# Attention and a dense mixture of experts on one core: Strassen blocks of 768 and 1024 tokens, and the keys' sums of two heads in two PSUM banks

## The chip, the cores and the metric

One core of a Trainium2 chip runs the whole program. The metric is device time in microseconds (us) for one execution; three runs of the kernel before gave 921.0, 921.02 and 921.77 us, median 921.02 us. The engines that the text speaks of are PE (matrix multiplications, with PEld for its weight loads), DVE, ACT and POOL (elementwise work) and SP (which only issues DMAs here). PE accumulates in PSUM, which has eight banks; each holds 512 float32 values per partition.

## The reference

Random-feature attention over 4 batches, 8 heads, 576 tokens, 64 values per head and 128 features; its output, 2304 tokens by 512, goes through four experts that every token uses, weighted by normalized probabilities:

```python
q_p, k_p = phi(q * s), phi(k * s)      # exp(x @ omega.T - |x|^2/2 - max) / sqrt(128)
kv  = einsum('bhsm,bhsd->bhmd', k_p, v);  z = sum(k_p, axis=2)
x   = (q_p @ kv) / (q_p @ z + 1e-6)    # 2304 tokens x 512
p   = probs / (probs.sum(-1) + 1e-9)
out = sum over 4 experts e:  p[:, e] * (relu(x @ w1[e]) @ w2[e])   # hidden width 1024
```

## The kernel before

**Precision.** A float32 operand of the expert layers is split into a high part and a rest, both of type fp32r, and each product is three matrix multiplications: high by high, high by rest, rest by high. Attention's sums over keys use plain float32; the trace counts each float32 multiplication as two PE instructions.

**The experts' visits.** The work is a list of visits (`visits`, L443 to L448). A visit takes a block of tokens and one half of an expert's hidden width (512, in four chunks `FH`); there are `NV` = 8 halves. The first 512 tokens are visited plainly. The other 1792 tokens are two blocks, u = 1 and u = 2, of `BIG` = 896 tokens each, and their first layer is done by Strassen's scheme: `build(u)` (L641) cuts the block in two halves of n = 448 tokens, forms seven combinations of the four quarters of x and splits each (`halve`: ACT writes the high part `xbh`, DVE the rest `xbl`). `sides` forms the combinations of w1. `fast(v)` (L677) runs one visit: for two groups g of hidden columns seven products, each of six multiplications with n = 448 moving columns (L694), that is 84 a visit; then `outputs` (L573 to L580), the second layer, token tile by token tile (128 tokens): four chunks by three multiplications with 512 moving columns, so 12 for each of the seven tiles, again 84 a visit. `keep` and `both` (L700 to L707) add the products on ACT and DVE and write the hidden values `hh` and `hl`; `gather` (L582) adds an output tile into `acc` on DVE. The products of a visit stand in PE's program before its outputs, but the outputs of the first three tiles begin between the last products (`begun`).

**Attention beside the experts.** Attention of later batches is cut into small steps (`later_ticks`, L386); a loop at the end of the kernel (`emit`) places a fixed number of steps for each share of a visit. Batch 4 (its four pairs of heads) is placed in the visits of u = 1; the visits of u = 2 have no attention beside them. `sum_keys` (L307) sums over the 576 keys of a pair of heads: one multiplication with all 128 rows and 256 columns for the tails of both heads (L311, the last 64 keys of either head on 64 of the rows, with zeros and ones laid out in `vb`), then four with 128 columns for either head (L315), all into one PSUM bank; ACT (L317) and DVE (L318) write the two parts of the result.

**What sets the order.** Each engine runs its instructions in the order in which the code is written; buffers come from rings (`bufs`), so an instruction that writes a new tile of a ring waits for the last readers of the old one. PSUM is one ring of eight banks for all uses (`bank`). The attention output `raw_x` is a ring of `RING` = 1344 tokens. `build(2)` runs in the last visit of u = 1.

## Time and profile before

| | |
|---|---|
| median of three runs | 921.02 us |
| the profiled execution | 921.18 us, span 919.4 us from first to last instruction |
| PE, weight load | 902.4 us (98%), 779.5 us (85%) |
| DVE, ACT, POOL busy | 551.2 us (60%), 431.4 us (47%), 379.1 us (41%) |
| granted TensorE clock | 0.999 of full speed |
| DMA | 83.56 MB, mean 91 GB/s |

A multiplication's record is longer than the distance to the next one, because they are pipelined: 128x448 has a mean of 366 ns, but one starts about every 203 ns. The cost of a multiplication on PE is therefore read from starts, not from durations. The visits of u = 1 lie between about 304.5 and 626.7 us of the span, those of u = 2 from there to the end.

### The profile page before, as it was taken

Reading aid. Unit: us, or ns where it says so; the run is one execution under the profiler, and the core shown is the slowest. Engines: PE = TensorE matmul, PEld = TensorE weight load, DVE = VectorE, ACT = ScalarE, POOL = GpSimd, SP = SyncE. Lnnn points to the kernel's source line nnn. Section 1 sums busy time; section 2 is a strip of 40 time slices with the busy share of each in tenths; the row PEclk is TensorE's granted clock in tenths of the full one; section 3 lists DMA queues with packets and bytes.
Section 4 is the critical chain, followed back from the end, with each engine's and each line's share of the span. In section 5 each row is a group of like instructions: output and inputs, shape, how many; then the busy total and the mean of one; then the engine's idle time right before and its main releaser. Section 6 shows DMA issues by size and latency. Waiting matters only on the chain.

```text
span 919.4 us, 13210 instructions
## 1 busy us (share of the span) xinstructions
PE 902.4 (98%) x4892; PEld 779.5 (85%) x4892; DVE 551.2 (60%) x945; ACT 431.4 (47%) x964; POOL 379.1 (41%) x296
## 2 busy tenths in 40 slices
PE   7999999999999999999999999999999999999998
PEld 7888887878887888888888889888888888888886
DVE  5665666776769665565666574877345545535543
ACT  4554566655655455435454445354444242343330
POOL 3856454443534443423434323445333433444330
PEclk9999999999999999999999999999999999999999
DMA  6664444444420523214123212215112122121102
GB/s 170 164 193 152 132 129 138 154 139 138 158 81 24 165 88 98 72 32 132 41 63 98 70 30 63 61 55 147 47 47 71 47 68 69 46 70 58 35 12 80
DMA packets 47360, 83.56 MB, mean 91 GB/s; under 512 B 8704, under 2 KB 17088, under 8 KB 47296
## 3 DMA queue, kind: packets, MB, share of 16 engines
q1 hardware_dynamic: 47056, 82.43, 29.8%
q8 instruction: 38, 0.62, 0.3%
q10 hardware_dynamic: 240, 0.30, 0.1%
q14 instruction: 26, 0.21, 0.1%
HBM read 77.99 MB, written 4.72 MB: 90 GB/s over the span
## 4 chain that ended last, share of the span: by engine, by line
PE 79%; DVE 10%; ACT 6%; issue 2%; DMA 1%; POOL 1%; SPq 0%; ACTq 0%; DVEq 0%; POOLq 0%
PE g L694 28%; PE g L578 12%; PE g L580 12%; PE g L579 12%; DVE dn L364 2%; PE g L563 2%; PE g L564 2%; PE g L565 2%; PE kv L315 2%; DVE acc L591 1%; ACT qp L297 1%; DVE raw_x L368 1%; PE q_ps L266 1%; ACT kp L297 1%; PE k_ps L266 1%
## 5 line engine op out<-in xcount | busy, mean ns | idle before, releaser
L578 PE MATMUL g<-w2h,hh 128*128 128x512 f32 x536 | 212.6, 397 | 0.0
L475 POOL TENSOR_TENSOR w2l<-w2r,w2h 128x512 fp32r<-128x512 f32 x93 | 122.2, 1318 | 217.9 <-ACT w2h L472 156.7
L580 PE MATMUL g<-w2h,hl 128*128 128x512 f32 x536 | 209.6, 391 | 0.8 <-DVE hl L570 0.8
L579 PE MATMUL g<-w2l,hh 128*128 128x512 f32 x536 | 209.0, 390 | 0.0
L475 POOL TENSOR_TENSOR w1sl<-w1r,w1sh 128x1024 fp32r<-128x1024 f32 (+1 forms) x59 | 113.2, 1922 | 152.9 <-ACT w1sh L472 138.1
L591 DVE SCALAR_TENSOR_TENSOR acc<-g,pr,acc 128x512 f32<-128x512 f32 x126 | 93.8, 748 | 66.2 <-PE g L580 65.3
L705 DVE TENSOR_TENSOR sum<-g,sum 128x448 f32<-128x448 f32 x96 | 59.7, 622 | 111.7 <-PE g L694 108.8
L475 POOL TENSOR_TENSOR w1al<-w1r,w1ah 128x256 fp32r<-128x256 f32 (+1 forms) x77 | 82.4, 1088 | 99.9 <-ACT w1ah L472 97.6
L580 PEld LDWEIGHTS g<-w2h,hl 128*128 128x128 f32 x536 | 100.6, 188 | 23.9 <-DVE hl L570 1.7
L578 PEld LDWEIGHTS g<-w2h,hh 128*128 128x128 f32 x536 | 100.7, 188 | 20.8 <-issue 1.4
L579 PEld LDWEIGHTS g<-w2l,hh 128*128 128x128 f32 x536 | 100.8, 188 | 18.6
L706 ACT ACTIVATE hh<-sum 128x448 fp32r<-128x448 f32 x96 | 55.5, 578 | 122.8 <-DVE sum L705 122.8
L707 DVE SCALAR_TENSOR_TENSOR hl<-sum,hh 128x448 fp32r<-128x448 f32 x96 | 61.8, 644 | 62.0 <-ACT hh L706 62.0
L472 ACT ACTIVATE w1sh<-w1r 128x1024 fp32r<-128x1024 f32 (+1 forms) x59 | 51.1, 867 | 100.0 <-DVE w1r L529 99.8
L694 PE MATMUL g<-xbh,w1sh 128*128 128x448 f32 x256 | 93.7, 366 | 0.7 <-ACT sum L700 0.7
L694 PE MATMUL g<-xbl,w1sh 128*128 128x448 f32 x256 | 93.7, 366 | 0.0
L694 PE MATMUL g<-xbh,w1sl 128*128 128x448 f32 x256 | 93.4, 365 | 0.0
L700 ACT ACTIVATE sum<-g 128x448 f32<-128x448 f32 x96 | 51.7, 541 | 56.2 <-PE g L694 56.0
L694 PE MATMUL g<-xbh,w1ah 128*128 128x448 f32 x192 | 70.6, 368 | 0.8 <-ACT kp L297 0.8
L694 PE MATMUL g<-xbh,w1al 128*128 128x448 f32 x192 | 70.3, 366 | 0.0
L694 PE MATMUL g<-xbl,w1ah 128*128 128x448 f32 x192 | 70.1, 365 | 0.0
L472 ACT ACTIVATE w2h<-w2r 128x512 fp32r<-128x512 f32 x90 | 55.7, 626 | 5.2 <-DMA w2r<-in_w 4.0
(158 smaller groups left out, 1597.1 us busy)
## 6 DMA issues: line engine op xcount, KB each, us to landing
w1r<-in_w SPq DMA_DIRECT2D x54, 512.0 KB, 3.6
w2r<-in_w SPq DMA_DIRECT2D x108, 256.0 KB, 2.7
out<-acc SPq DMA_DIRECT2D x18, 256.0 KB, 2.6
va<-in_vn SPq DMA_DIRECT2D x14, 256.0 KB, 4.7
k<-in_kd SPq DMA_DIRECT2D x12, 288.0 KB, 3.1
k<-in_kn SPq DMA_DIRECT2D x12, 288.0 KB, 4.4
q<-in_qd SPq DMA_DIRECT2D x12, 288.0 KB, 4.3
q<-in_qn SPq DMA_DIRECT2D x12, 288.0 KB, 4.7
```

The lines of the kernel that those rows point to most:

```text
L266: nc.tensor.matmul(ps[j][:, cs], t[rows, cs], om_r[rows], start=True, stop=True)
L472: hi.activation(a, t, AF.Copy)
L475: lo.tensor_tensor(c, t, f32(a), ALU.subtract)
L578: nc.tensor.matmul(ps, ha[:, ts_], wa, start=(c == 0), stop=False)
L579: nc.tensor.matmul(ps, ha[:, ts_], wc, start=False, stop=False)
L580: nc.tensor.matmul(ps, hc[:, ts_], wa, start=False, stop=(c == FH - 1))
L591: nc.vector.scalar_tensor_tensor(acc[i], ps, sc, acc[i], ALU.mult, ALU.add)
L694: nc.tensor.matmul(ps, a[:, w], x[:, k], start=(start and k + at == 0), stop=(k == 1 and at == 2), skip_group_check=not start)
L700: nc.scalar.activation(t, P_[g][where], AF.Copy)
L705: nc.vector.tensor_tensor(t, P_[g][where], t, ALU.add)
L706: nc.scalar.activation(ha, t, AF.Relu)
L707: nc.vector.scalar_tensor_tensor(hc, t, 0.0, f32(ha), ALU.max, ALU.subtract)
```

## The change

- The blocks have 768 tokens (u = 1, from token 512) and 1024 tokens (u = 2, from token 1280). A product's moving operand has 384 columns in u = 1 and 512 in u = 2; the number of products, of multiplications in each, and of output tiles over both blocks (6 + 8 where it was 7 + 7) is the same.
- In u = 2 the hidden values of the second 512 tokens live in tiles that attention used before (`k`, `q`, `kp`, `qp`), and the eighth accumulator in a tile of `qt`. To make room, the ring of attention output has 1280 tokens, the first block's two parts share one tile, and the query tails have one buffer where they had two.
- In `build`, the rest of combinations 3 and 4 is written by POOL where DVE wrote it.
- `sum_keys` has a bank for each head. The tails are two multiplications, each on its head's 64 rows with 128 columns, one into each bank; then the four of each head as before. ACT and DVE evacuate each bank by itself.
- The rate of attention steps in u = 1 follows the smaller number of tiles.

```diff
@@ exp_tails (Halves), exp (Pair)
-            f = att.tile([P, 1, M], F32, tag=which + "pt", name=which + "p", bufs=2)
+            f = att.tile([P, 1, M], F32, tag=which + "pt", name=which + "p", bufs=2 if which == "k" else 1)
...
@@ finish
-                x_first[self.hp] = [xop([P, START], x) for x in ("xh", "xl")]
+                both = xop([P, 2, START], "x_first")
+                x_first[self.hp] = both[:, 0], both[:, 1]
@@ sum_keys
-            kv = bank("kv")[:, :VZ]
-            nc.tensor.matmul(kv, self.kp[2][:, 0], vb[:, self.hp], start=True, stop=False)
+            kv = [bank("kv")[:, :P] for _ in range(2)]
+            cs = [slice((1 - j) * P, (2 - j) * P) for j in range(2)]
             for j in range(2):
-                cs = slice((1 - j) * P, (2 - j) * P)
+                rows = slice(j * D, (j + 1) * D)
+                nc.tensor.matmul(kv[j], self.kp[2][rows, 0], vb[rows, self.hp, cs[j]], start=True, stop=False)
+            for j in range(2):
                 for t in range(4):
-                    nc.tensor.matmul(kv[:, cs], self.kp[j][:, t], va[:, t, cs], start=False, stop=(j == 1 and t == 3))
+                    nc.tensor.matmul(kv[j], self.kp[j][:, t], va[:, t, cs[j]], start=False, stop=(t == 3))
             self.kv_h, self.kv_l = (att.tile([P, VZ], F32R, tag=x, name=x, bufs=1) for x in ("kvh", "kvl"))
-            nc.scalar.activation(self.kv_h, kv, AF.Copy, scale=1.0 / M)
-            nc.vector.scalar_tensor_tensor(self.kv_l, kv, 1.0 / M, f32(self.kv_h), ALU.mult, ALU.subtract)
+            for j in range(2):
+                hi, lo = self.kv_h[:, cs[j]], self.kv_l[:, cs[j]]
+                nc.scalar.activation(hi, kv[j], AF.Copy, scale=1.0 / M)
+                nc.vector.scalar_tensor_tensor(lo, kv[j], 1.0 / M, f32(hi), ALU.mult, ALU.subtract)
@@ visits
-    BIG = 7 * P
+    BIG = {1: (START, 6 * P), 2: (START + 6 * P, 8 * P)}
-    visits += [visit(u, n, START + (u - 1) * BIG, BIG) for u in (1, 2) for n in range(NV)]
+    visits += [visit(u, n, *BIG[u]) for u in (1, 2) for n in range(NV)]
@@ build
-            split(t, *X[p], nc.scalar, nc.vector)
+            split(t, *X[p], nc.scalar, nc.gpsimd if p in (3, 4) else nc.vector)
@@ fast
-        u, n = visits[v][0], BIG // 2
-        tiles = BIG // P
-        hs = [tuple(held([P, 2 * n], x) for x in ("hh", "hl")) for _ in range(FH)]
+        u, _, _, _, n = visits[v]
+        tiles, n = n // P, n // 2
+        if u == 1:
+            whole = [tuple(held([P, 2 * n], x) for x in ("hh", "hl")) for _ in range(FH)]
+            hs = [[tuple(x[:, j * n:(j + 1) * n] for x in pair) for pair in whole] for j in range(2)]
+        else:
+            wide = [att.tile([P, 2, n], F32R, tag=x, name="h_" + x, bufs=1) for x in "kq"]
+            late = [tuple(x[:, i] for i in range(2)) for x in wide]
+            late += [tuple(att.tile([P, n], F32R, tag=x, name="h_" + x, bufs=2) for _ in range(2)) for x in ("kp", "qp")]
+            hs = [[tuple(held([P, n], x) for x in ("hh", "hl")) for _ in range(FH)], late]
...
@@ emit
-            N0: (chain(opening(later[-NP]), later_ticks(later[-NP:])), 54 / (NV * (BIG // P + 1) * 0.8)),
+            N0: (chain(opening(later[-NP]), later_ticks(later[-NP:])), 54 / (NV * 7 * 0.8)),
```

**The end of the products in a visit of u = 1, on PE.** The last product of a visit stands beside the outputs of a tile (`g` is a PSUM bank, `xbh` and `xbl` the split combination of x, `w1sh` and `w1sl` that of w1). Before:

```order
L694 MATMUL g_3616<-xbh,w1sh 128x448
L694 MATMUL g_3616<-xbl,w1sh 128x448
L694 MATMUL g_3616<-xbh,w1sl 128x448
L578 MATMUL g_3696<-w2h,hh 128x512
L579 MATMUL g_3696<-w2l,hh 128x512
L580 MATMUL g_3696<-w2h,hl 128x512
```

and now:

```order
L712 MATMUL g_3644<-xbh,w1sh 128x384
L712 MATMUL g_3644<-xbl,w1sh 128x384
L712 MATMUL g_3644<-xbh,w1sl 128x384
L585 MATMUL g_3724<-w2h,hh 128x512
L586 MATMUL g_3724<-w2l,hh 128x512
L587 MATMUL g_3724<-w2h,hl 128x512
```

The order is the same, and only the width of the products has changed, to 384 here and to 512 in u = 2; there are 672 of either width where there were 1344 of 448.

**The sum over keys of a pair, on PE**, between the multiplications of a plain visit (the numbers behind `kv` tell banks apart, `kp` are the keys' features, `va` and `vb` the values and ones). Before:

```order
L565 MATMUL g1_1256<-xh_543,w1al_1048 128x512
L311 MATMUL kv_1288<-vb_77,kp_1206 128x256
L315 MATMUL kv_1288<-va_76,kp_1180 128x128 x4
L315 MATMUL kv_1288<-va_76,kp_1201 128x128 x4
L563 MATMUL g1_1304<-xh_427,w1sh_1086 128x512
```

and now:

```order
L570 MATMUL g1_1252<-x_first_540,w1al_1044 128x512
L315 MATMUL kv_1284<-vb_77,kp_1202 128x128
L315 MATMUL kv_1285<-vb_77,kp_1202 128x128
L318 MATMUL kv_1284<-va_76,kp_1176 128x128 x4
L318 MATMUL kv_1285<-va_76,kp_1197 128x128 x4
L568 MATMUL g1_1304<-x_first_427,w1sh_1082 128x512
```

The two multiplications of the tails work on 64 rows each, and stand one behind the other ahead of those with all rows; nothing has moved past another stage.

**POOL in the last visit of u = 1** (rests of the split weights, `w1al`, `w1sl`, `w2l`). Before:

```order
L475 TENSOR_TENSOR w1al<-w1r,w1ah 128x512
L475 TENSOR_TENSOR w1al<-w1r,w1ah 128x256
L475 TENSOR_TENSOR w1sl<-w1r,w1sh 128x1024 x2
L475 TENSOR_TENSOR w2l<-w2r,w2h 128x512 x4
```

and now:

```order
L480 TENSOR_TENSOR w1al<-w1r,w1ah 128x512
L480 TENSOR_TENSOR w1al<-w1r,w1ah 128x256
L480 TENSOR_TENSOR w1sl<-w1r,w1sh 128x1024
L480 TENSOR_TENSOR xbl<-raw_x,xbh 128x1024
L480 TENSOR_TENSOR w1sl<-w1r,w1sh 128x1024
L480 TENSOR_TENSOR xbl<-raw_x,xbh 128x1024
L480 TENSOR_TENSOR w2l<-w2r,w2h 128x512 x4
```

Two splits of x stand in POOL's queue, one ahead of the second `w1sl` and one ahead of the four `w2l`; they are gone from DVE's.

## Rows read from the trace of the kernel before

**Rows 1.** The page: span, and PE's busy time, share, instructions.

```profile
span 919.4 us, 13210 instructions
...
PE 902.4 (98%) x4892; PEld 779.5 (85%) x4892; DVE 551.2 (60%) x945; ACT 431.4 (47%) x964; POOL 379.1 (41%) x296
```

**Rows 2.** Windows: length, busy of PE, PEld, DVE, ACT, POOL, clock, DMA.

```profile
304.50:626.70 322.20, 320.72 (x1649) 277.20 (x1649) 207.12 (x341) 152.23 (x319) 124.47 (x89) 1.00 0.25 76
590.00:630.00 40.00, 39.47 (x184) 33.99 (x183) 32.01 (x40) 20.09 (x33) 18.39 (x12) 1.00 0.27 79
626.70:915.40 288.70, 288.70 (x1345) 252.11 (x1343) 138.16 (x220) 108.36 (x194) 105.68 (x75) 1.00 0.20 59
```

**Rows 3.** Waits of PE: in total us, times, longest us.

```profile
PE qt_ps L326 <- ACT qp L297: 2.2, 3, 1.3
...
PE nd L356 <- DVE qtl L337: 1.2, 3, 0.8
...
PE g L694 <- ACT kp L297: 0.8, 1, 0.8
PE g L694 <- ACT sum L700: 0.7, 2, 0.5
```

**Rows 4.** The chain in time: start, length of a stretch, products in it.

```profile
382.89 13.63 PE g L694 x66
...
626.84 13.38 PE g L694 x66
```

**Rows 5.** Timeline of PE, 256 columns: first and last of 22.

```profile
56.43 0.28 PE L565 MATMUL g<-xh,w1sl 128*128 128x256 f32 x1
...
58.94 0.28 PE L565 MATMUL g<-xh,w1al 128*128 128x256 f32 x1
```

**Rows 6.** Timeline of PE, 320 columns: first of six, and what follows.

```profile
132.03 0.31 PE L354 MATMUL nd<-qth,kvh 128*128 128x320 f32 x1
...
132.91 0.39 PE L578 MATMUL g<-w2h,hh 128*128 128x512 f32 x1
```

**Rows 7.** Timeline of PE, 512 columns and w1: first and last of 13.

```profile
283.85 0.39 PE L565 MATMUL g<-xh,w1al 128*128 128x512 f32 x1
...
286.57 0.39 PE L565 MATMUL g<-xh,w1sl 128*128 128x512 f32 x1
```

**Rows 8.** Timeline of PE around one sum over keys.

```profile
97.24 0.39 PE L565 MATMUL g<-xh,w1al 128*128 128x512 f32 x1
97.47 0.59 PE L311 MATMUL kv<-vb,kp 128*128 128x256 f32 x2
97.89 1.95 PE L315 MATMUL kv<-va,kp 128*128 128x128 f32 x16
99.60 0.47 PE L563 MATMUL g<-xh,w1sh 128*128 128x512 f32 x1
99.91 0.39 PE L564 MATMUL g<-xl,w1sh 128*128 128x512 f32 x1
```

**Rows 9.** Timeline of PE around multiplications on 64 rows.

```profile
91.84 0.39 PE L565 MATMUL g<-xh,w1sl 128*128 128x512 f32 x1
92.16 1.16 PE L266 MATMUL q_ps<-om_r,q 64*128 64x128 f32 x16
93.25 0.50 PE L563 MATMUL g<-xh,w1sh 128*128 128x512 f32 x1
93.59 0.39 PE L564 MATMUL g<-xl,w1sh 128*128 128x512 f32 x1
```

**Rows 10.** Lines by form: busy us, mean ns, idle before, releaser.

```profile
L694 PEld LDWEIGHTS g<-xbh,w1sh 128*128 128x128 f32 x256 | 48.1, 188 | 6.3 <-ACT sum L700 1.4
...
L317 ACT ACTIVATE kvh<-kv 128x256 fp32r<-128x256 f32 x12 | 4.6, 380 | 1.4 <-PE kv L315 1.2
...
L318 DVE SCALAR_TENSOR_TENSOR kvl<-kv,kvh 128x256 fp32r<-128x256 f32 x12 | 5.1, 424 | 16.5 <-ACT kvh L317 16.5
...
L475 DVE TENSOR_TENSOR xbl<-raw_x,xbh 128x896 fp32r<-128x896 f32 x10 | 14.1, 1417 | 6.8 <-ACT xbh L472 6.8
...
L475 POOL TENSOR_TENSOR w1sl<-w1r,w1sh 128x1024 fp32r<-128x1024 f32 x32 | 78.3, 2446 | 127.6 <-ACT w1sh L472 113.3 <-DVE acc L591 10.5 <-PE g L579 3.9
```

More of the change, by code (lines that the diff above doesn't have):

```diff
@@ L34, in attention_moe @@
     QS = float(D) ** -0.25
-    RING = 1344
+    RING = 1280
     START = 4 * P
@@ L158, in exp @@
             else:
-                f = att.tile([P, n, M], F32, tag=which + "p" + size, name=which + "p", bufs=2)
+                f = att.tile([P, n, M], F32, tag=which + "p" + size, name=which + "p", bufs=1 if which + size == "qt" else 2)
             for i in range(n):
@@ L573, in outputs @@
     def outputs(v, hs, ps, t, cs):
+        at = t * P // hs[0][0][0].shape[1]
+        hs, t = hs[at], t - at * hs[0][0][0].shape[1] // P
         ts_ = slice(t * P, (t + 1) * P)
@@ L587, in gather @@
         if n_tiles[i] == 1:
-            acc[i] = held([P, DM], "acc", F32)
+            if t < 7:
+                acc[i] = held([P, DM], "acc", F32)
+            else:
+                acc[i] = att.tile([P, DM], F32, tag="qt", name="acc")
             nc.scalar.activation(acc[i], ps, AF.Copy, scale=sc)
@@ L623, in plain @@
             ps = bank("g2")
-            outputs(v, hs, ps, t, range(2))
+            outputs(v, [hs], ps, t, range(2))
             if v == N0 - 2 and t in (0, 2):
@@ L629, in plain @@
             yield 0.5
-            outputs(v, hs, ps, t, range(2, FH))
+            outputs(v, [hs], ps, t, range(2, FH))
             gather(v, ps, t)
@@ L641, in build @@
     def build(u):
-        c0, n = START + (u - 1) * BIG, BIG // 2
+        c0, n = BIG[u]
+        n //= 2
         o = [(c0 + j * n - START) % RING for j in range(2)]
@@ L677, in fast @@
     def fast(v):
-        u, n = visits[v][0], BIG // 2
-        tiles = BIG // P
-        hs = [tuple(held([P, 2 * n], x) for x in ("hh", "hl")) for _ in range(FH)]
+        u, _, _, _, n = visits[v]
[3 more added lines that the diff above has]
+            hs = [[tuple(x[:, j * n:(j + 1) * n] for x in pair) for pair in whole] for j in range(2)]
+        else:
+            wide = [att.tile([P, 2, n], F32R, tag=x, name="h_" + x, bufs=1) for x in "kq"]
+            late = [tuple(x[:, i] for i in range(2)) for x in wide]
+            late += [tuple(att.tile([P, n], F32R, tag=x, name="h_" + x, bufs=2) for _ in range(2)) for x in ("kp", "qp")]
+            hs = [[tuple(held([P, n], x) for x in ("hh", "hl")) for _ in range(FH)], late]
         P_ = [{}, {}]
@@ L702, in both @@
         def both(g, f, j, where, name):
-            ha, hc = (x[:, j * n:(j + 1) * n] for x in hs[2 * g + f])
+            ha, hc = hs[j][2 * g + f]
             t = P_[g][name]
@@ L730, in p4 @@
             product(g, 4, "u", start=False)
-            ha, hc = (x[:, :n] for x in hs[2 * g + 1])
+            ha, hc = hs[0][2 * g + 1]
             nc.scalar.activation(ha, P_[g]["u"], AF.Relu)
@@ L927, in first_visit @@
             ps = bank("g2")
-            outputs(0, hs, ps, t, range(FH))
+            outputs(0, [hs], ps, t, range(FH))
             gather(0, ps, t)
```

## The prediction

> **What bounds the kernel now.** The page comes first: PE is busy for 902.4 of 919.4 us [rows 1], so only two things can move the end by much: how long PE needs for its own stream, or new waits in it. The windows say where the slack lies. In u = 2 PE is busy for all of its 288.7 us; in u = 1 it is idle for 322.20 - 320.72 = 1.48 us; DVE, the next engine, is busy for 207 of those 322 us [rows 2]. The waits of PE are short: the longest kinds in the stages that the change touches add up to 2.2, 1.2, 0.8 and 0.7 us [rows 3]. So no wait is there to be removed, and the change is worth what it does to the distance between starts of PE's instructions, less what it adds in waits. I therefore went from busy time to the timeline and read starts, since records of pipelined multiplications overlap.
>
> **The products' width.** 1344 products of 448 columns become 672 of 384 and 672 of 512: the same columns, and the same number of instructions. Whether that costs nothing, gives or takes depends on what a start costs beyond its columns. The granted clock is 1.00 [rows 2], the level of 2.4 GHz, at which 448 columns need 186.7 ns. The chain holds 66 products in 13.38 us, 202.7 ns each, so 16.0 ns lie on top [rows 4]. For other widths: 256 columns, 21 steps in 2.51 us, 119.5 ns, 12.8 on top of 106.7 [rows 5]; 320 columns, 6 steps in 0.88 us, 146.7 ns, 13.4 on top [rows 6]; 512 columns, 12 steps in 2.72 us, 226.7 ns, 13.4 on top of 213.3 [rows 7]. The last group has w1 standing and x moving, as the products have, so it is the right row for the new 512. The width of 448 stands out by 2.6 ns.
>
> For 384 no row exists. By the neighbours 320 and 512 it takes 160.0 + 13.4 = 173.4 ns; with the surplus of 448 it takes 176.0 ns. It is 64 columns from 320 and 64 from 448, so I take the middle, 174.7 ns. Before: 1344 x 202.7 ns = 272.4 us. After: 672 x 174.7 ns + 672 x 226.7 ns = 117.4 + 152.3 = 269.7 us. That is -2.7 us, all of it on PE, which is the path; the ends are -3.6 us (173.4 ns) and -1.8 us (176.0 ns). A further end, at which the 512 columns too carry 16.0 ns, is 0 and is a rival below. One stretch of u = 1 runs at 13.63 us for 66 products [rows 4], 3.8 ns more each; I don't know why. Two visits at that pace cost 2 x 84 x 3.8 ns = 0.6 us, which may stay or go; I count nothing for it.
>
> The outputs stay at 12 multiplications for a tile and 14 tiles over both blocks, and cost what they did.
>
> **The tails of the keys' sums.** Before, the multiplication with 256 columns takes the path from 97.47 to 97.89, 0.42 us [rows 8]. The new two have 64 rows and 128 columns, the form of the projection of queries: there 16 instructions take 1.09 us, 0.068 us each, and the new two are four instructions, 0.27 us [rows 9]. But the projection also pays at its edges. The step into it is 92.16 - 91.84 = 0.32 us, where a step behind 512 columns is 0.23: 0.09 us more. The step after it is 0.34, 0.11 more; a sum over keys, which has all 128 rows, has 0.31 there, 0.08 more [rows 8, 9], so leaving the 64 rows is worth 0.03. With both edges the new tails take 0.09 + 0.27 + 0.03 = 0.39 us. That saves 0.03 us in each of 12 pairs, -0.4 us. The ends: no edge paid, 12 x (0.27 - 0.42) = -1.8 us; the whole 0.11 paid on leaving, 12 x (0.47 - 0.42) = +0.6 us. I take the middle value, since the row has the form of the new instructions and shows the edge.
>
> The Trainium skill, TensorEngine Tiling (Array Packing), Key Properties, says the same against this edit: "Changing tiling mode (not just tile) drains the TensorE". The trace agrees, with the 0.09 us of the step in; without that rule and that row the sum would hold -1.8 us here instead of -0.4.
>
> **The two banks.** ACT's evacuation (380 ns for 256 columns) becomes two of 128, DVE's (424 ns) likewise [rows 10]. Each piece costs between half and all of the old one, so ACT gets 0 to 0.38 us and DVE 0 to 0.42 us more a pair. They lie beside PE's work: the sum is first read in `numerators`, three steps later, behind two transposing steps and expert multiplications. Value 0; if that cover were gone, up to 0.8 us a pair. A pair now takes 12 tiles of the ring of eight banks where it took 11, while a visit of u = 1 takes one fewer for its outputs. Queued behind a product that waits for a bank is all of PE.
>
> **The splits moved to POOL.** In the last visit of u = 1 DVE is the busiest helper (32.0 of 40 us in 590 to 630) and POOL has 18.4 of 40 [rows 2]. Two rests, 1.42 us each on DVE, leave it; on POOL a rest of 1024 elements takes 2.45 us [rows 10]. Behind the first stands the second `w1sl`, which the eighth product of the next visit reads: seven products, 7 x 6 x 0.2267 = 9.5 us after that visit's start, and that covers 2.45 us. The rests themselves are read by the ninth and tenth product. The four `w2l` behind them are read by outputs later still. Value 0, in `build(1)` too; without the cover 2.45 us once or twice.
>
> **Denser visits of u = 1.** A visit loses 84 x 28 ns = 2.35 us of products and a tile of 12 x 0.2267 = 2.72 us, so u = 1 shrinks by about 41 to 282 us, with the same attention and weights beside it. DVE's 207 us would be at most 73% of that, from 64%. PE's idle 1.48 us there [rows 2] may vanish or double: -1.5 to +1.5 us. I take +0.3, a fifth more, for the higher density. The buffers that become single (query tails) or shared (first block, hidden values in attention's tiles) are rewritten one pair or visit after their last read, behind PE's own later work: 0.
>
> **Sum.** -2.7 - 0.4 + 0.3 = -2.8 us. The profiled execution took 921.18 us (span 919.4 and 1.8 around it), so 918.4 us; it lies 0.16 above the median of the runs, which puts the forecast at 918.2 us. With ends of its terms near each other its own range is 916.8 to 919.6.
>
> **Rivals.**
> - *Columns alone count.* What lies on top belongs to the products, not to 448: 384 and 512 both carry 16.0 ns, 672 x (176.0 + 229.3) = 272.4 us, a gain of 0; the time is 921.0 - 0.4 + 0.3 = 920.9 us. For it: only the products have the 16 ns. Against it: the 512 columns with w1 standing carry 13.4 [rows 7]. Chance 0.17. The Trainium skill, TensorE: Matmul & The Clock Gate, Back-to-back issue gap, gives a gap of columns at 2.4 GHz plus a fixed 2.5 ns for the warm array; by that rule 384 and 512 cost on average what 448 does, and this rival holds. The rows disagree with it in size (12.8 to 16.0 ns) and in being fixed.
> - *Both gains whole.* 384 as its neighbours and the tails without edges: -3.6 - 1.8 = -5.4, 915.6 us. Rows 9 speak against the second half. Chance 0.14.
> - *The half rows do nothing.* The edges eat the tails (+0.6), the rest as forecast: 919.2 us. Chance 0.05.
> - *A wait for banks.* A product in u = 1 finds its bank still held by features that ACT has not finished; one such wait is 0.8 us now [rows 3]. If each of 12 pairs pays it for the additional bank: +9.6, 918.2 + 9.6 = 927.8 us. It ends on the slower side from (2.8 + 1.8) / 12 = 0.4 us a pair. Against it: one such wait in the whole run now, and one output bank fewer a visit. Chance 0.06.
> - *Weight loads become the bound.* A load's record is 188 ns [rows 10], just under the 202.7 of a product; if loads set the pace, 384 stays at 202.7: 672 x 28 ns = +18.8, 937 us. It ends slower once 384 takes 181.5 ns or so. Against it: with the same kind of load 256 columns start every 119.5 ns [rows 5]. Chance 0.03.
>
> **How the numbers follow.** The forecast has 0.55. A measurement of this kernel tells 0.2%, 1.84 us, from no change, so faster begins at 919.2 us. The forecast is below that in about four of five of its cases (0.44); with the whole gains (0.14), half of the third rival and a little of the first that makes 0.62 faster. The first rival, the rest of the forecast and of the third make 0.29 within, and the two last 0.09 slower. A range of 915.2 to 921.4 leaves out the two slow rivals (0.09) and the far side of the whole gains.
>
> **What would show it.** In the changed trace 66 products of u = 1 should stretch over 66 x 174.7 ns = 11.5 us (11.4 to 11.6), and those of u = 2 over 15.0 us; 15.1 and 11.6 mean the first rival, 13.4 in u = 1 the weight loads. From the start of the tails to that of the sums with all rows it should be 0.27 to 0.30 us, after a step of 0.32 into them. PE's waits in u = 1 should stay under 3 us in all, u = 2 without any, and no wait should name `xbl` on POOL. Wrong is the forecast if the 448 columns' 16 ns turn up at 512 too, or if PE's waits there grow by more than 2 us.

## The result, and the profile after

The changed kernel takes 932.21 us (median of six, 930.48 to 936.32) against 921.38 us for the kernel before in the same comparison (six, 920.86 to 924.14): ratio 1.012, 95% interval 1.0093 to 1.0147. The prediction said 918.2 us and put slower at 0.09. The profiled execution after took 930.67 us with a span of 928.9 us; the one before had 919.4 us [rows 1].

The page of the kernel after, span and busy time of each engine:

```profile
span 928.9 us, 13300 instructions
PE 904.0 (97%) x4916; PEld 769.6 (83%) x4916; DVE 554.1 (60%) x953; ACT 430.8 (46%) x976; POOL 390.2 (42%) x300
```

PE's busy time is about what it was (904.0, before 902.4), and the span is 9.5 us longer: 7.9 us of that are idle time of PE. The windows say where (columns as in [rows 2]):

```profile
302.50:555.00 252.50, 246.78 (x1394) 218.96 (x1393) 162.11 (x294) 124.82 (x289) 104.97 (x78) 1.00 0.27 84
555.00:605.00 50.00, 44.73 (x206) 38.57 (x206) 42.25 (x50) 24.63 (x40) 29.89 (x15) 0.97 0.28 86
605.00:925.00 320.00, 320.00 (x1407) 263.75 (x1405) 145.78 (x221) 111.74 (x187) 102.61 (x74) 1.00 0.17 51
573.00:575.00 2.00, 2.00 (x8) 2.00 (x7) 1.49 (x2) 0.67 (x3) 2.00 (x1) 0.50 0.00 0
```

From 605 us on PE is never idle. In the 50 us around the border between u = 1 and u = 2 it is idle for 5.3 us, and in the 252 us before that for 5.7 us. The fourth row lies inside the second one: a busy PE at a granted clock of 0.50, the level of 1.2 GHz. No stretch of u = 1 or u = 2 in [rows 2] is below 1.00.

PE's waits in the kernel after (columns as in [rows 3]):

```profile
PE g L712 <- ACT sum L718: 5.4, 5, 2.1
PE g L712 <- DVE sum L723: 2.5, 1, 2.5
PE g L585 <- DVE raw_x L373: 1.6, 1, 1.6
PE t_ps L274 <- DVE raw_x L373: 1.1, 1, 1.1
```

Before, a product waited for ACT's `sum` for 0.7 us in all [rows 3]; it is 5.4 now. The chain gives the pace of the products (columns as in [rows 4]), one stretch of u = 1 and one of u = 2:

```profile
373.75 11.45 PE g L712 x66
...
638.32 14.96 PE g L712 x66
```

That is 173.5 ns for 384 columns and 226.7 ns for 512, against 202.7 for 448 [rows 4]: 672 x 173.5 + 672 x 226.7 = 268.9 us, 3.5 us less than 272.4.

To see which visits lost time I took the distance between the first products of neighbouring visits (us; the eighth is the distance to the first visit of u = 2). The first product of u = 1 starts at 301.89 us before and at 300.78 after. "Planned" is the row of before less 84 x 29.2 ns and 12 x 0.2267 us, 5.17 us a visit:

| visit of u = 1 | 1 | 2 | 3 | 4 | 5 | 6 | 7 | 8 | sum |
|---|---|---|---|---|---|---|---|---|---|
| before | 38.48 | 42.36 | 42.45 | 42.67 | 43.02 | 40.77 | 37.82 | 37.22 | 324.8 |
| planned | 33.31 | 37.19 | 37.28 | 37.50 | 37.85 | 35.60 | 32.65 | 32.05 | 283.4 |
| after | 35.31 | 37.50 | 38.46 | 38.30 | 38.91 | 36.27 | 32.69 | 37.37 | 294.8 |

So 11.4 us of the shrinking did not come: 5.3 in the eighth visit, 2.0 in the first, 4.0 spread over the others. In u = 2 a visit was to take 36.11 + 84 x 24.0 ns + 2.72 = 40.85 us; the first takes 42.56 and the seven others 40.99, so 2.7 us more than planned in all. With 1.1 us less ahead of u = 1 (the start of the program differs by some us from profile to profile) the difference of the spans is closed: -3.5 + 11.4 + 2.7 - 1.1 = +9.5 us.

**The eighth visit, its border.** Timeline of the kernel after around 558 us, from the outputs of the visit before into the new products (start, length, engine, line, out<-in, tile; in brackets the idle time before it and its releaser), by engine:

```profile
557.29 2.67 POOL L480 TENSOR_TENSOR w1sl<-w1r,w1sh 128x1024 fp32r<-128x1024 f32 x1 [8.55 <-ACT w1sh L477]
...
557.29 0.41 DVE L531 TENSOR_TENSOR w1r<-w1r 128x256 f32<-128x256 f32 x1
557.74 2.50 DVE L532 TENSOR_TENSOR w1r<-w1r 128x256 f32<-128x256 f32 x1
...
560.73 0.43 DVE L534 TENSOR_TENSOR w1r<-w1r 128x256 f32<-128x256 f32 x1
...
561.25 1.06 ACT L477 ACTIVATE w1sh<-w1r 128x1024 fp32r<-128x1024 f32 x1 [4.04 <-DVE w1r L534]
562.22 0.47 ACT L718 ACTIVATE sum<-g 128x384 f32<-128x384 f32 x1
...
558.22 0.33 PE L712 MATMUL g<-xbh,w1ah 128*128 128x384 f32 x1
...
562.74 0.44 PE L712 MATMUL g<-xbh,w1sh 128*128 128x384 f32 x1 [1.21 <-ACT sum L718]
```

Four engines form one chain. DVE adds the quarters of the next w1 (L531 to L534); one of the four additions takes 2.50 us instead of 0.42 while POOL writes `w1sl`: it ends at 560.24, 0.28 us after POOL's instruction (559.96). That is the rule in this trace: of the 128 additions of w1, 16 take 0.60 to 2.51 us; each of them started while a POOL instruction was running and ended 0.28 to 0.29 us after it. The other 112 take 0.41 to 0.43. DVE is held here, not slowed. ACT's split of the result (L477) waits for the last addition. ACT's copy of the first product (L718) needs nothing of that, but stands behind the split in ACT's queue. And PE's fourth product of the visit adds onto the bank that this copy reads, so PE stops. Three products of six multiplications each pass before the fourth, 18 x 173.5 ns = 3.1 us; the copy starts 4.0 us after the visit's first product. Less the 2.1 us for which the addition was held it would be 1.9 (an estimate from these rows), inside the 3.1. The same chain costs 2.12 us in the first visit of u = 1 and 1.28 in the first of u = 2, and there too an addition is held (1.41 us at 301.84, 1.96 at 595.13).

The same border in the kernel before:

```profile
585.74 0.41 DVE L526 TENSOR_TENSOR w1r<-w1r 128x256 f32<-128x256 f32 x1
...
587.62 1.06 ACT L472 ACTIVATE w1sh<-w1r 128x1024 fp32r<-128x1024 f32 x1 [5.19 <-DVE w1r L529]
590.94 0.55 ACT L700 ACTIVATE sum<-g 128x448 f32<-128x448 f32 x1 [2.25 <-PE g L694]
...
589.46 0.36 PE L694 MATMUL g<-xbh,w1ah 128*128 128x448 f32 x1
```

There the additions start 3.7 us ahead of the visit's first product (0.9 after), the split is over before that product starts, and ACT's copy waits for PE, not PE for ACT.

**The eighth visit, the second block.** DVE and PE a little later, in the kernel after:

```profile
565.12 2.31 DVE L663 TENSOR_TENSOR t_k<-raw_x 128x1024 f32<-128x1024 f32 x1
567.46 2.20 DVE L663 TENSOR_TENSOR t_q<-raw_x,t_k 128x1024 f32<-128x1024 f32 x1
...
571.19 0.55 DVE L723 TENSOR_TENSOR sum<-g,sum 128x384 f32<-128x384 f32 x1
...
571.79 0.44 PE L712 MATMUL g<-xbh,w1ah 128*128 128x384 f32 x1 [2.54 <-DVE sum L723]
...
572.35 0.52 PE L712 MATMUL g<-xbh,w1al 128*128 128x384 f32 x1
572.67 0.52 PE L712 MATMUL g<-xbh,w1ah 128*128 128x384 f32 x1
```

Two combinations of x for the second block stand in DVE's queue ahead of the sums that free PE's banks, 4.5 us long where the two took 3.1 before (1.08 and 2.06). Their size is the smaller part of it: a subtraction of 1024 elements that POOL does not hold takes 1.22 us (at 572.80), one of 896 took 1.08. Before, POOL held one of the two, and now it holds both, with two `w2l` (564.73 to 568.58). PE waits 2.54 us, and then the multiplications start 0.32 us apart instead of 0.174: this is the window at 0.50 above. Twelve at that distance take 12 x 0.146 = 1.75 us more; whether the visit is longer by it, the fourth experiment shows.

**The sum over keys.** In the kernel after, beside [rows 8]:

```profile
406.31 0.39 PE L587 MATMUL g<-w2h,hl 128*128 128x512 f32 x1
406.63 0.49 PE L315 MATMUL kv<-vb,kp 64*128 64x128 f32 x4
407.05 2.05 PE L318 MATMUL kv<-va,kp 128*128 128x128 f32 x16
...
409.18 0.39 PE L586 MATMUL g<-w2l,hh 128*128 128x512 f32 x1
```

From the last multiplication ahead of the block to the second behind it: 2.87 us, before 2.67. The step in is 0.32 instead of 0.23, the tails take 0.42 as they did, and from there to the second multiplication behind the block it is 2.13 instead of 2.02, since the 16 sums take 0.10 more. Together that is +0.20 us a pair, and for 12 pairs +2.4 us. Ten of the 12 pairs show it so; at 194.73 us the tails take 0.75, and behind the pair at 119.91 PE waits:

```profile
123.14 0.38 PE L568 MATMUL g<-x_first,w1ah 128*128 128x256 f32 x1 [0.76 <-ACT qp L298]
```

The expert's multiplication reads nothing of `qp`; by the code only the ring of banks ties it to ACT's exponentials.

### The profile page after: what moved, and what is told of

It is laid out like the page before. It is cut to its first block, busy times and chain, and to the rows that moved or that the text cites. A ratio compares the mean times of both kernels' runs of the same rounds, so it can differ in the third digit from the quotient of the medians.

```text
span 928.9 us, 13300 instructions
## 1 busy us (share of the span) xinstructions
PE 904.0 (97%) x4916; PEld 769.6 (83%) x4916; DVE 554.1 (60%) x953; ACT 430.8 (46%) x976; POOL 390.2 (42%) x300
## 4 chain that ended last, share of the span: by engine, by line
PE 77%; DVE 11%; ACT 6%; issue 3%; POOL 1%; DMA 0%; ACTq 0%; DVEq 0%; POOLq 0%
PE g L712 27%; PE g L585 12%; PE g L587 11%; PE g L586 11%; PE g L568 2%; PE g L569 2%; PE g L570 2%; DVE dn L369 2%; PE kv L318 2%; DVE acc L601 1%; ACT qp L298 1%; PE q_ps L267 1%; PE k_ps L146 1%; DVE raw_x L373 1%; PE k_ps L267 1%
## 5 line engine op out<-in xcount | busy, mean ns | idle before, releaser
L585 PE MATMUL g<-w2h,hh 128*128 128x512 f32 x408 | 162.4, 398 | 1.6 <-DVE raw_x L373 1.6
L587 PE MATMUL g<-w2h,hl 128*128 128x512 f32 x408 | 159.6, 391 | 0.3 <-DVE hl L575 0.3
L723 DVE TENSOR_TENSOR sum<-g,sum 128x384 f32<-128x384 f32 (+1 forms) x96 | 59.7, 622 | 108.7 <-PE g L712 103.7
L712 PE MATMUL g<-xbh,w1sh 128*128 128x384 f32 (+1 forms) x256 | 93.6, 366 | 5.6 <-ACT sum L718 5.4
L477 ACT ACTIVATE w1sh<-w1r 128x1024 fp32r<-128x1024 f32 (+1 forms) x59 | 51.1, 867 | 97.7 <-DVE w1r L534 97.6
L712 PE MATMUL g<-xbl,w1sh 128*128 128x384 f32 (+1 forms) x256 | 93.0, 363 | 0.0
L712 PE MATMUL g<-xbh,w1sl 128*128 128x384 f32 (+1 forms) x256 | 92.9, 363 | 0.0
L718 ACT ACTIVATE sum<-g 128x384 f32<-128x384 f32 (+1 forms) x96 | 51.5, 539 | 64.2 <-PE g L712 63.6
L712 PE MATMUL g<-xbh,w1ah 128*128 128x384 f32 (+1 forms) x192 | 70.3, 366 | 2.8 <-DVE sum L723 2.5
L712 PE MATMUL g<-xbh,w1al 128*128 128x384 f32 (+1 forms) x192 | 69.9, 364 | 0.0
L712 PE MATMUL g<-xbl,w1ah 128*128 128x384 f32 (+1 forms) x192 | 69.8, 363 | 0.0
L712 PEld LDWEIGHTS g<-xbh,w1sh 128*128 128x128 f32 x256 | 48.3, 189 | 13.5 <-ACT sum L718 7.2
```

Source lines behind the costliest of these rows:

```text
L477: hi.activation(a, t, AF.Copy)
L585: nc.tensor.matmul(ps, ha[:, ts_], wa, start=(c == 0), stop=False)
L587: nc.tensor.matmul(ps, hc[:, ts_], wa, start=False, stop=(c == FH - 1))
L712: nc.tensor.matmul(ps, a[:, w], x[:, k], start=(start and k + at == 0), stop=(k == 1 and at == 2), skip_group_check=not start)
L718: nc.scalar.activation(t, P_[g][where], AF.Copy)
L723: nc.vector.tensor_tensor(t, P_[g][where], t, ALU.add)
```

## The experiments

Each ratio is against the kernel before, run on the same chip; the kernel after has 1.012.

**One bank again** (`e1_one_bank`): the changed kernel with the old `sum_keys`.

```diff
-            kv = [bank("kv")[:, :P] for _ in range(2)]
...
+            kv = bank("kv")[:, :VZ]
+            nc.tensor.matmul(kv, self.kp[2][:, 0], vb[:, self.hp], start=True, stop=False)
```

> The changed kernel with the sum over keys of before: one bank, one multiplication of 128 rows and 256 columns for the tails. Theory edges (the step into and out of the 64 rows costs PE 0.20 us a pair: the block from the last expert multiplication ahead of it to the second behind it takes 2.87 us in the changed kernel and 2.67 before): 12 x 0.20 = 2.4 us faster than the changed kernel, nothing else moves. Theory ring (the twelfth bank of a pair makes PE meet banks that DVE's divisions still hold: 1.6 + 1.1 us of waits on raw_x, which before had none): these 2.7 us go as well, 5.1 us in all. Rival (both are chance of placement): 0 to 1 us. The 5.4 us of waits on ACT's copies of product sums stay by all three.

931.94 us, ratio 1.012 (1.0106 to 1.0135): no difference that can be told. In its trace u = 1 is 294.1 us long (after 294.8), 0.18 us for each of its four pairs, and every wait of PE above is still there with its length, the 2.5 us and the two of `raw_x` among them. So the additional bank is not their cause. It moves a wait in the plain visits: the 0.76 us behind the second pair are gone here, and those of `qt_ps` for ACT's `qp` are 2.3 us, as before (2.2), where the kernel after has 0.9. All PE's waits from 90 to 295 us add up to 3.7 us here and 3.2 in the kernel after.

**Two banks alone** (`e2_two_banks_alone`): the kernel before with the new `sum_keys` and nothing else (the same lines with the signs exchanged).

```diff
-            kv = bank("kv")[:, :VZ]
+            kv = [bank("kv")[:, :P] for _ in range(2)]
```

> The kernel before with the new sum over keys alone (blocks stay 896 and 896). Theory edges: 12 x 0.20 = 2.4 us slower than before, 923.8 us, with PE's waits as before. Theory ring: waits on raw_x or other evacuations appear beside it, some 2 to 3 us more. The prediction's step (0.03 us a pair saved): 0.4 us faster.

922.67 us against 920.96, ratio 1.0018 (1.0009 to 1.0027): slower by 1.7 us. The pair of [rows 8] in its timeline:

```profile
96.48 0.39 PE L569 MATMUL g<-xh,w1al 128*128 128x512 f32 x1
96.80 0.49 PE L314 MATMUL kv<-vb,kp 64*128 64x128 f32 x4
97.22 2.05 PE L317 MATMUL kv<-va,kp 128*128 128x128 f32 x16
...
99.35 0.39 PE L568 MATMUL g<-xl,w1sh 128*128 128x512 f32 x1
```

2.87 us again. The half rows cost time in either kernel, and that they should save 0.4 us falls. The wait behind the second pair is there too (0.77 us), and PE's idle time in u = 1 stays at 1.5.

**The sums of w1 group by group, two steps sooner** (`e3_sides_early`).

```diff
...
+        for i in range(2):
+            direct(i)
+            yield
+            add(i)
+            yield
+            summed(i)
+            yield
@@ fast
         p7(1)
+        next(ready, None)
@@
         begun(2)
+        next(ready, None)
```

> The changed kernel with the combinations of the next visit's w1 made group by group and two steps sooner (direct, add, summed of group 0, two of them between the last products; then those of group 1 in the first three output tiles). Theory border (at the end of a visit of six tiles ACT stands at the split of w1sh, waiting for DVE's adds, with the copy of the first product of the next visit queued behind it, and PE's third product waits for that copy): the waits of 2.1, 1.2 and 1.3 us at the starts of visits go, about 5 us faster than the changed kernel. Rival (DVE has too much to do in those places, wherever the adds stand): the waits move to sums or hidden values, less than 1.5 us gained.

939.54 us, ratio 1.0208 (1.0192 to 1.0223): a miss in the total. The eighth visit shrank from 37.37 to 34.72 us and the first of u = 2 from 42.56 to 41.20, as the chain would have it, but the fourth grew from 38.30 to 42.57, where PE waits 3.4 us for `raw_x`, and the first from 35.31 to 39.05, where the wait for ACT's `sum` stays (2.2) and DMAs of `k` and `q` are waited for (1.1 and 0.8). Too much moved at once.

**Rests of combinations 3 and 4 on DVE again** (`e4_halves_dve`).

```diff
-            split(t, *X[p], nc.scalar, nc.gpsimd if p in (3, 4) else nc.vector)
+            split(t, *X[p], nc.scalar, nc.vector)
```

> The changed kernel with all rests of x's combinations on DVE, none on POOL. Theory pool (POOL's rests lengthen DVE's instructions beside them: a DVE add of w1 took 1.96 to 2.50 us there instead of 0.43): DVE gets shorter in all, and 1 to 3 us are gained at the start of u = 2. Rival (DVE is the short engine there, POOL has time): two rests of 1.2 to 2.6 us come back to DVE, and the first visits of u = 1 and u = 2 lose 1 to 3 us.

930.82 us, ratio 1.0108 (1.0094 to 1.0122). The medians do not tell it from the kernel after, but the trace does: the first visit of u = 1 takes 33.77 us instead of 35.31, the other visits what they took. The rests on POOL cost that border 1.5 us: beside them DVE's third rest took 2.59 us (here 0.95) and the first addition of w1 1.41 (here 0.41). The rest of 2.51 us ahead of these is as long here, beside POOL's `w1sl`.

Its eighth visit settles what the slow clock cost (timeline of PE, and the window of the fourth row above):

```profile
571.86 0.44 PE L712 MATMUL g<-xbh,w1ah 128*128 128x384 f32 x1 [2.54 <-DVE sum L723]
...
573.00:575.00 2.00, 1.93 (x11) 1.45 (x9) 1.56 (x2) 0.67 (x2) 2.00 (x1) 1.00 0.00 0
```

The wait is the same 2.54 us, the granted clock behind it is 1.00, and the visit takes 37.38 us, as in the kernel after (37.37). PE is through the next products sooner and waits 0.61 and 0.66 us for ACT instead of 0.24. So the slow clock lay over time that PE would have waited anyway.

**A higher rate of attention steps in the kernel before** (`e5_rate_before`).

```diff
-            N0: (..., 54 / (NV * (BIG // P + 1) * 0.8)),
+            N0: (..., 54 / (NV * (BIG // P + 1) * 0.7)),
```

> The kernel before with one number changed: attention's steps are placed in u = 1 at 54 / (8 x 8 x 0.7) = 1.21 a share, the changed kernel's rate, instead of 1.05; blocks stay 896 and 896. Theory density (what makes PE wait in u = 1 of the changed kernel is how many steps stand beside one output tile): waits on raw_x and on ACT's copies turn up in u = 1, 2 to 4 us slower than before. Rival (the shorter products are what uncovers them, the steps don't matter): within 1 us of before.

924.09 us against 920.69, ratio 1.0032 (1.002 to 1.0044): +3.4 us with wide products, all seven tiles and one bank. Its waits:

```profile
PE g L694 <- ACT sum L700: 1.5, 2, 1.0
PE t_ps L273 <- DVE raw_x L368: 1.1, 1, 1.1
```

The wait for `raw_x` of 1.1 us is that of the kernel after. So density has a price of its own, which the prediction put at 0.3.

**A lower rate in the kernel after** (`e6_rate_after`).

```diff
-            N0: (..., 54 / (NV * 7 * 0.8)),
+            N0: (..., 54 / (NV * 7 * 0.87)),
```

> The changed kernel with the steps placed at 54 / (8 x 7 x 0.87) = 1.11 a share instead of 1.21. Theory density: the waits of 1.1 and 1.6 us on raw_x go, 2 to 3 us faster than the changed kernel, unless the last steps run into the build of the second block. Rival (short products): unchanged within 1 us.

937.2 us, ratio 1.0172 (1.0146 to 1.0199): slower, a miss for density as the whole story. The waits for `raw_x` went down to 0.6 us, but those of products grew:

```profile
PE g L712 <- ACT sum L718: 10.6, 6, 3.0
```

Three visits that had no wait at their fourth product now wait 2.96, 2.49 and 1.23 us there. So what counts seems to be which steps fall on a border; which ones did here was not followed up.

**The additions of w1 on POOL** (`e7_adds_pool`), for the visits of u = 1.

```diff
+            eng = nc.gpsimd if N0 < v <= N0 + NV else nc.vector
-            nc.vector.tensor_tensor(r22, r21, r22, ALU.add)
+            eng.tensor_tensor(r22, r21, r22, ALU.add)
```

(and so the three lines that follow)

> The changed kernel with the adds that combine w1 on POOL for the visits prepared during u = 1 (eight adds of 128x256 a visit, 0.43 us each on DVE when nothing slows them). Theory DVE short (DVE's queue at the output tiles is what ACT's split of w1sh and the release of banks wait for): the waits on raw_x and part of those on ACT's copies go, 3 to 6 us faster than the changed kernel. Rival (it is the chain from adds over ACT to PE, or DVE and POOL slowing each other): POOL takes about 0.8 us for each add, the split comes later still, 0 to 5 us slower.

934.83 us, ratio 1.0146 (1.013 to 1.0163). Products now wait 8.8 us for ACT's `sum`, and the second visit takes 42.44 us instead of 37.50, the first of u = 2 45.43 instead of 42.56; others are shorter, the eighth at 34.79. On POOL an addition takes 0.74 to 0.80 us in the mean. At the second border ACT's split starts at 340.48 us, 1.7 us behind the visit's first product, and exponentials of attention stand between it and the copy at 344.80. Moved to POOL, the additions are no way out.

**One combination of the second block later** (`e8_less_later`).

```diff
         p1(1)
-        next(more, None)
         p2(1)
+        next(more, None)
```

> The changed kernel with one step of the second block's build moved in the last visit of u = 1, from ahead of the second product of group 1 to behind it, so that the two first subtractions (2.31 and 2.20 us on DVE) no longer stand together ahead of that product's sum. Theory queue (those 4.5 us make the wait of 2.54 us on DVE's sum, and the clock's drop to 1.2 GHz behind it): that wait and the slow products behind it go, 3 to 4 us faster than the changed kernel. Rival (the work is only put off): the wait moves to the seventh product or the hidden values, under 1 us gained.

930.7 us, ratio 1.0109 (1.0091 to 1.0127). The eighth visit takes 36.30 us instead of 37.37. PE's waits there:

```profile
571.21 0.44 PE L712 MATMUL g<-xbh,w1ah 128*128 128x384 f32 x1 [1.45 <-DVE sum L723]
...
574.89 0.49 PE L585 MATMUL g<-w2h,hh 128*128 128x512 f32 x1 [0.63 <-ACT hh L750]
...
576.74 0.44 PE L712 MATMUL g<-xbh,w1sh 128*128 128x384 f32 x1 [0.67 <-ACT sum L718]
```

The wait for DVE's `sum` falls from 2.54 to 1.45 us, and the granted clock stays at 1.00. But the products that now run at full pace meet waits of 0.63 and 0.67 us right behind, where the kernel after had 0.24. So 1.1 us are gained, which is what the wait lost: as in the fourth experiment, the slow clock had lain over waits that come without it.

**One step sooner** (`e9_step_sooner`): the next visit's weights are advanced once more in each visit of u = 1, ahead of its outputs, and by one step in the last plain visit.

```diff
-            if f != 1:
-                next(ready, None)
+            next(ready, None)
@@ fast
         begun(2)
+        if u == 1:
+            next(ready, None)
```

> The changed kernel with the making of the next visit's w1 combinations one step sooner in u = 1 and in the last plain visit, in the same order: the last adds and the last split of w1sh have two output tiles behind them again, as they had with seven tiles, where the changed kernel has one. Theory border (the tile that the visit lost was the cover of the chain from DVE's adds over ACT's split to ACT's copy of the next visit's first product): the waits of 2.1, 0.5, 1.2 and 1.3 us on ACT's copies at starts of visits go, 4 to 5 us faster than the changed kernel; the waits on raw_x and on the second block's subtractions stay. Rival (DVE and ACT have too much to do beside six tiles, wherever the chain stands): such waits turn up at other visits or at the hidden values, under 1.5 us gained.

925.87 us against 920.58, ratio 1.0062 (1.0047 to 1.0076): 5 to 6 us of the loss are gone. Its waits, and the border of the eighth visit:

```profile
PE g L711 <- DVE sum L722: 1.3, 1, 1.3
...
PE g L711 <- ACT sum L717: 0.7, 1, 0.7
```

```profile
557.80 0.41 DVE L531 TENSOR_TENSOR w1r<-w1r 128x256 f32<-128x256 f32 x1
...
559.17 0.43 DVE L534 TENSOR_TENSOR w1r<-w1r 128x256 f32<-128x256 f32 x1
...
559.69 1.06 ACT L477 ACTIVATE w1sh<-w1r 128x1024 fp32r<-128x1024 f32 x1 [8.28 <-DVE w1r L534]
560.72 0.49 ACT L717 ACTIVATE sum<-g 128x384 f32<-128x384 f32 x1
...
559.39 0.33 PE L711 MATMUL g<-xbh,w1ah 128*128 128x384 f32 x1
```

The wait for ACT's `sum` falls from 5.4 to 0.7 us. The additions stand 1.6 us ahead of the first product and none is stretched; the copy starts 1.3 us behind that product instead of 4.0. The chain at the border is shown as a cause, in the changed kernel. Two things went together, though: the additions come sooner, and none of them meets POOL's `w1sl` any more; how much belongs to either is not separated.

**One step later in the kernel before** (`e10_step_later`).

```diff
             gather(v, g2[t], t)
-            next(ready, None)
+            if u > 1 or t:
+                next(ready, None)
```

> The kernel before (seven tiles, 896 and 896) with those steps one tile later in u = 1, so that one tile stands behind the last of them, as in the changed kernel. Theory border: waits on ACT's copies of 1 to 3 us turn up at the starts of several visits of u = 1, as in the changed kernel, 3 to 6 us slower than before. Rival: at most 1 us slower, since seven tiles leave DVE and ACT time enough.

921.74 us against 920.58, ratio 1.0015 (1.0002 to 1.0028): 1.2 us, and PE's waits for ACT's `sum` stay at 0.7. Only the eighth visit is longer, 38.73 instead of 37.22. The rival held: with wide products and seven tiles a step may slip. It is a weak test, since the additions slipped by less than a tile: one was stretched to 2.50 us here too (586.00 to 588.50), but 2.6 us ahead of the first product at 588.61, where the kernel after has its own 0.5 us ahead. With that lead a held addition makes no wait at the border. The eighth visit has two new waits further on, 0.41 us for DVE's `sum` at 600.13 and 0.47 for ACT's `hh` at 603.98; they explain part of its 1.5 us.

**Four edits together** (`e11_mended`): the edits of the first, fourth, eighth and ninth experiment in the changed kernel.

```diff
+            kv = bank("kv")[:, :VZ]
...
+            split(t, *X[p], nc.scalar, nc.vector)
...
+        if u == 1:
+            next(ready, None)
```

> The changed kernel's blocks of 768 and 1024 tokens with four of its costs taken away at once: the sum over keys of before, all rests of x on DVE, the w1 steps one sooner as in the run before this, and one subtraction of the second block's build behind the second product of group 1. If the costs add up (2.4, 1.5, 4 to 5, and 1 us) it takes some 9 us less than the changed kernel, 921 to 922 us, level with the kernel before; theory border puts it there. The rival leaves it at 925 us or more.

927.01 us, ratio 1.0069 (1.0057 to 1.0081), no better than the ninth alone. u = 1 is 2.0 us shorter than there (288.2 against 290.2), but the first visit of u = 2 takes 44.96 us instead of 40.99:

```profile
591.61 2.59 DVE L476 TENSOR_TENSOR xbl<-raw_x,xbh 128x1024 fp32r<-128x1024 f32 x1 [0.34 <-ACT xbh L473]
...
597.02 0.68 DVE L718 TENSOR_TENSOR sum<-g,sum 128x512 f32<-128x512 f32 x1
...
599.90 0.77 PE L707 MATMUL g<-xbh,w1sh 128*128 128x512 f32 x1 [2.08 <-ACT sum L713]
```

DVE's rests of the second block now stand ahead of the first `sum`, ACT's `hh` waits for that, ACT's copy stands behind `hh`, and PE stops for 2.08 us: the same kind of chain with another producer. From 600 to 602 us the granted clock is 0.50. At the first border the rests on DVE bring nothing any more: the first visit of u = 1 takes 33.25 us here and 32.92 in the ninth experiment, with two of them on POOL.

**The same without the rests on DVE** (`e12_mended_pool`): the edits of the first, eighth and ninth experiment in the changed kernel.

```diff
+            kv = bank("kv")[:, :VZ]
...
+        p2(1)
         next(more, None)
-        p2(1)
...
+        if u == 1:
+            next(ready, None)
```

> The run with the w1 steps one sooner, plus the sum over keys of before and the one subtraction of the second block's build behind the second product of group 1; two rests of x stay on POOL. If what the earlier runs showed adds up: 2.4 us less for the sums over keys' edges and about 1 us less for the subtraction than the run with the steps alone, 922 to 923 us, still 1 to 3 us slower than the kernel before: left are waits on divisions and on exponentials at output tiles (about 3 us) and the hidden values in attention's tiles (1.4 us). Rival (the repairs cost each other, as when the rests went back to DVE): 925 us or more.

923.15 us (eight runs, 920.76 to 923.86) against 920.22, ratio 1.0028 (1.0017 to 1.0038). u = 1 takes 287.8 us and u = 2 has 40.99 in every visit, so with the step sooner it is the rests on POOL that help at the border to u = 2 (44.96 in the run before this). The two waits for `raw_x` are left, at 1.1 and 0.9 us, with some shorter ones.

No version that was run beats the kernel before. From the first product of u = 1 on, its trace is 2.0 us longer than that of the kernel before: -3.5 for the products, 287.8 - 283.4 = +4.4 in u = 1, and 8 x 0.14 = +1.1 in u = 2. The trace is that of the fastest of the eight executions, in which u = 1 starts 2.4 us sooner (299.46 us instead of 301.89); what makes up the 2.9 us of the medians is not shown further.

**Hidden values in exchanged tiles** (`e13_tiles_swapped`, one execution): the ninth experiment's kernel with hidden chunks 0 and 1 of the second half in `kp` and `qp`, 2 and 3 in `k` and `q`.

```diff
-            late += [tuple(att.tile(...) ...) for x in ("kp", "qp")]
+            late = [tuple(att.tile(...) ...) for x in ("kp", "qp")] + late
```

> The run with the w1 steps one sooner, with the tiles of u = 2's second hidden half exchanged: chunks 0 and 1 in the tiles kp and qp, chunks 2 and 3 in k and q. In u = 2 of the changed kernel a visit takes 40.99 us where 84 products and 96 output multiplications at 226.7 ns make 40.81, and the records of those that read h_kp are 395 to 404 ns, those on h_k 389. Theory tile (where the tile lies makes the reading slower): the long records stay with h_kp, and a visit stays at 40.99. Theory chunk (it is the place in the sequence): they go over to h_k, and a visit stays at 40.99. If both are wrong a visit drops to 40.8.

924.34 us for the one run; a visit of u = 2 takes 40.99 us as before. Multiplications of its outputs by form in u = 2 (busy us, mean ns of one, idle):

```profile
L587 PE MATMUL g<-w2h,hl 128*128 128x512 f32 x112 | 43.6, 389 | 0.0
L585 PE MATMUL g<-w2h,h_kp 128*128 128x512 f32 x27 | 10.9, 404 | 0.0
L587 PE MATMUL g<-w2h,h_kp 128*128 128x512 f32 x27 | 10.7, 397 | 0.0
```

The records of 397 and 404 ns stayed with the tile `kp` although other chunks lie in it. The tile makes the difference, not the chunk. Starts say the same as records, in the kernel after and here: the three multiplications that read `kp` start 241, 233 and 236 ns ahead of the next one, those of `qp` 228, 233 and 231, the one just ahead of `kp` 233, and the others 227. In the kernel after that is 0.046 us for each of the four token tiles of the second half, the 0.18 us of a visit. What about these tiles makes it, is open.

## Why the prediction was wrong

**Right: the products' width.** 384 columns take 173.5 ns (said: 174.7, between 173.4 and 176.0) and 512 take 226.7. The term is -3.5 us (said -2.7). 448 was the dear width, and the rivals of columns alone and of weight loads both fall. Nearly right: the two banks cost nothing on balance. One wait for a bank did come, as the rival had it, but 0.76 us in a plain visit and not one for each of 12 pairs, and other waits became shorter by more (first experiment).

**Mis-sized: the tails.** -0.4 us was said, +0.6 as the worst end; it is +0.20 x 12 = +2.4 us in the rows, and 1.7 us in the median of the second experiment. The step in came as read from [rows 9] (0.32). But I took the inside from there as well, 0.27 us for four instructions of a row of 16; these four take 0.42, and the 16 sums behind them 0.10 more. A short run of another shape is nearly all edge. The Trainium skill, TensorEngine Tiling (Array Packing), Key Properties, says that a change of the tiling mode drains TensorE; the rows agree that the change costs, and it weighed more than I let it.

**The step that failed: "Denser visits of u = 1", +0.3 us (-1.5 to +1.5).** I took a share of busy time, DVE at 73%, and scaled the idle time that was there. u = 1 lost 11.4 us. PE's idle time there went from 1.48 to 9.7 us (5.7, and 5.3 without the 1.3 that belongs to u = 2); the slower clock, which took the place of other waits, makes 1.75 of the rest and the edges 0.8. The mechanism was missing from my rivals: I checked PSUM banks, buffers and rests, and for each only the tile itself, not what stands behind its producer in a queue. The weights' sums of the next visit run during the outputs of this one. A visit with six tiles has 2.72 us less of that time, and with narrow products the fourth product comes 18 x 29 ns = 0.5 us sooner. Behind the additions of DVE hangs ACT's split, behind that ACT's copy, and behind that PE. The ninth experiment shows this chain at 5 to 6 us; the fifth shows that density alone is worth 3.4 us on the kernel before. What the tile, the narrow products and POOL each do to the chain was not tried one by one. A late chain alone is not all of it: at the three longest waits on it an addition was held by POOL, and in the fourth experiment, where the additions at the first border start only 0.6 us ahead of the first product but none is held, the wait of 2.12 us is gone. Nor is a held addition alone: in the tenth, the kernel before with seven tiles, it has 2.6 us of lead, and PE does not wait for it.

**Failed: the rests on POOL at 0 in `build(1)` too.** I asked when the rest is read, and found 9.5 us of cover. It held: no wait names `xbl` on POOL, as the prediction said. But while POOL wrote them, they held one of DVE's own rests (2.59 us) and the first addition of w1 behind it (1.41), and through the chain PE waited 2.12 us. The fourth experiment shows 1.5 us.

**Failed: the second block's combinations, not named at all.** They went from 3.1 to 4.5 us together, a little by their size and mostly because POOL now holds both, and stand next to products that leave less time for the sums behind them. They cost 2.5 us of wait. The eighth experiment got 1.1 of that back; with the step sooner as well the eighth visit is down by 3.7 us, to 33.70 in the twelfth.

**Failed: that the outputs "cost what they did".** Half of them in u = 2 read attention's tiles; a visit takes 40.99 us where 180 multiplications of 0.2267 would be 40.81: 0.18 us a visit, 1.4 in all eight. The thirteenth experiment ties the longer records to the tiles.

**What stays open.** The kernel after has a median 1.5 us above its own profiled execution, and the rows account for the 9.5 us of its trace only. The granted clock goes with it: its mean is 0.998 in the two shortest of the six executions (930.48 and 930.67 us), 0.996 in the next three and 0.994 in the longest (936.32). So the longer ones ran at the lower level for more of their time; where, no trace shows. Why the clock fell after one wait of 2.54 us and not after the other is open, and so is the reason for the tiles `kp` and `qp`. The smaller ring of `raw_x`, the shared tile of the first block and the single query tails were not tried by themselves.

## What to carry to other kernels

Where PE is busy all the time, a shorter stretch of PE is also a shorter cover: follow each producer of the next stretch to what stands behind it in its queue, and measure its lead over the first reader of that, in us, before and after. A cover is lost at one border in full, not as a share of all idle time. Where one engine holds another up, as POOL does DVE here, add the longest hold to the chain. And a cheaper shape pays only where the run of it is long enough for its edges.

## What the hardware showed that was not expected

- Of the widths here, 448 columns cost 16.0 ns on top of their columns; 384 (13.5) and 512 (13.4) do not.
- After a wait of PE of 2.54 us the granted clock was 0.50 for some 3 us, and multiplications with 384 columns started every 0.32 us instead of 0.174; after the 2.08 us in the eleventh experiment it fell too. After the 2.12 us of the kernel after at 306 us it stayed at 1.00, and after the same 2.54 us in the fourth experiment as well.
- Entering 64 rows cost 0.09 us, and 16 sums with all rows behind them 0.10 us more than before; the two tails took the 0.42 us of the one multiplication that they replaced.
- An addition of 128x256 that DVE started while POOL was at work ended 0.28 us after POOL's instruction, and so took up to 2.51 us instead of 0.42 (16 of 128 in the kernel after, 15 in the kernel before); a rest of 128x768 took 2.51 instead of 0.95.
- A multiplication that reads the tile `kp` of SBUF had a record of 404 ns instead of 389 and came 241 ns ahead of the next instead of 227, whichever chunk lay in it.
